# Gated linear attention and a two-level mixture of experts: the attention in a fixed order on every engine

## The chip, the core and the metric

The kernel runs on one core of one Trainium2 chip. The core has a matrix engine (TensorE, PE in the profile; PEld is its weight load), a vector engine (VectorE, DVE), a scalar engine (ScalarE, ACT), a general one (GpSimd, POOL) and a queue engine that issues transfers (SyncE, SP). Each works through its own instructions in order and waits on semaphores of the others. The metric is the device time of one execution in microseconds (us).

## The reference

```python
for t in range(S):                       # gla_recurrent: B 4, H 8, S 768, D 48
    state = alpha[:, :, t, :, None] * state + np.einsum('bhd,bhe->bhde', k[:, :, t], v[:, :, t])
    y[:, :, t] = np.einsum('bhd,bhde->bhe', q[:, :, t], state)
x = y.transpose(0, 2, 1, 3).reshape(B * S, H * D)            # 3072 tokens of 384
g_idx = np.argmax(x @ w_group, axis=1); g_w = softmax(x @ w_group)[g_idx]     # 4 groups
e_idx = np.argmax(x @ w_expert[g], axis=1); e_w = softmax(...)[e_idx]         # 4 experts in a group
out = (g_w * e_w) * (np.maximum(x @ w1[g, e], 0) @ w2[g, e])                  # 384 -> 1024 -> 384
```

## The kernel before, in words

The attention is cut into chunks of 128 tokens: a step n is one chunk of one batch entry, all 8 heads, so there are 4 x 6 = 24 steps (n = 0 to 23), and the state of a batch entry is carried over its 6 steps. Two heads lie together as a pair p (partitions 0 to 47 and 64 to 111), four pairs in all. Inputs come in units of one, two and then three steps.

For a pair of a unit, `decayed` forms the running products of alpha by two scans on VectorE (`back`, L224, and `forth`, L230 and L232) and multiplies them into the keys and queries on GpSimd (`kp`, L227, `qp`, L234). A step then has: `scores` (L245, 8 matrix products into two PSUM banks, one for each head of the pairs, and two causal masks on VectorE, L248); `turned_keys` (transposes L260, copy `kt` on ScalarE, L261); `next_state` (L274, keys by values; the old state added, L281, and scaled by the decay of the chunk, L283, both on VectorE; two copies on ScalarE, L287, that put the heads as blocks on the diagonal of a 112 x 112 matrix); `outputs` (L297, state by queries, whole blocks; L302, masked scores by values; copy `yt` on ScalarE, L306); `to_rows` (L318, the outputs turned to rows of tokens and multiplied by the routers' weights `wr`; logits L321 on VectorE, rows `xr` on ScalarE, L324). An fp32 matrix product is two instructions in the trace, a transpose is one.

After the last step of a batch entry (for the last entry in three parts) `choose` picks group and expert (a chain of small VectorE operations) and `send` counts places and writes the tokens' rows to slots in DRAM, one scatter (L400, an indirect transfer that GpSimd issues) per chunk. Then 16 experts follow, 224 slots each, on the same tiles of weights; their part is not touched.

The order is written as a Python loop with a queue of portions (`later`, `spend`), but the compiler's own scheduler may still reorder the instructions of the attention on every engine. Transfers: SyncE issues `qka` (queries and keys, L194, and alpha, L192, apart) and the weights; ScalarE issues `wr` (L121) and `v` (L201). Scans of a pair write `cq`, of which there are two buffers, so a third scan waits for GpSimd's product of the first.

Of the kernel before, what the change touches and what calls it, by code (L numbers as in the profile page):

```python
# [2 lines left out]

# [21 lines left out]

@with_exitstack
def gla_then_hierarchical_moe(
    ctx: ExitStack,
    tc: tile.TileContext,
    qk_d: bass.AP,  # L30
    al_d: bass.AP,
# [23 lines left out]

    nc = tc.nc
    B, HP, R, SQ = qk_d.shape
    NC = SQ // (2 * P)
# [4 lines left out]
    UC = NC // 2  # L63
    A1 = P + 1
# [56 lines left out]
    nc.scalar.dma_start(out=wr, in_=wr_d)  # L121
# [3 lines left out]
    nc.vector.memset(blank, 0.0)  # L125
    nc.vector.memset(blank.rearrange("p (t w) -> p t w", t=2)[:, :, DM + 1:XW], float(N))
# [6 lines left out]
    nc.vector.tensor_copy(out=xr[:, :, DM + 1], in_=token_f)  # L133
# [13 lines left out]
    with ExitStack() as gla:  # L147
        buf = gla.enter_context(tc.tile_pool(name="buf", bufs=1))
        inp = gla.enter_context(tc.tile_pool(name="inp", bufs=6))
# [8 lines left out]
        state = [buf.tile([R, HP, D], F32, name=f"state{i}") for i in range(2)]  # L158
        blocks = [buf.tile([R, HP, R], F32, name=f"blocks{i}") for i in range(3)]
        for t in state + blocks:  # L160
            nc.vector.memset(t, 0.0)


        units = [(0, 0, 1), (0, 1, 2), (0, UC, UC)]
        units += [(b, c, UC) for b in range(1, B) for c in (0, UC)]
# [19 lines left out]
        def load(u):  # L185
            b, c0, k = units[u]
            o = 2 * k * P
# [10 lines left out]
        def load_v(b):  # L198
            vs[b] = prep.tile([P, NC, DM], F32, name="v")
            for c0, c1 in ((0, 1), (1, NC)) if b == 0 else ((0, NC),):  # L200
                nc.scalar.dma_start(out=vs[b][:, c0:c1].rearrange("p c e -> p (c e)"),  # L201
                                    in_=v_d[b, :, c0 * DM:c1 * DM])
# [35 lines left out]
        def scores(n):  # L238
            u, c = where[n]
            qp, kp, _ = ready[u]  # L240
            sm = work.tile([P, 2, HP, P], F32, name="sm")
            z = [bank() for _ in heads]
            for p in range(HP):
                for i, r in enumerate(heads):
                    nc.tensor.matmul(z[i][:, p * P:(p + 1) * P], lhsT=kp[r, p, c, :],  # L245
                                     rhs=qp[r, p, c, :], start=True, stop=True)
            for i in range(2):
                nc.vector.tensor_tensor(out=sm[:, i], in0=z[i].rearrange("p (h i) -> p h i", h=HP),  # L248
                                        in1=causal[:, None, :].to_broadcast([P, HP, P]),
                                        op=ALU.mult)  # L250
            return sm
# [12 lines left out]
        def next_state(n, kt):  # L264

            u, c = where[n]
            tot = ready[u][2][:, :, c, 0:1]
            z = bank()
            b, bc = divmod(n - 1, NC)
# [8 lines left out]
            old, new = state[(n + 1) % 2], state[n % 2]  # L278
            add = z[0:R, 0:HP * D].rearrange("r (p e) -> r p e", p=HP)
            if bc:  # L280
                nc.vector.tensor_tensor(out=new, in0=old, in1=add, op=ALU.add)  # L281
                add = new
# [5 lines left out]
            return blk  # L288

        def outputs(n, sm, blk):  # L290

            u, c = where[n]
            qp = ready[u][0]
            b, bc = divmod(n, NC)
            z = bank()
            for p in range(HP):
                nc.tensor.matmul(z[0:R, p * P:(p + 1) * P], lhsT=blk[:, p, :], rhs=qp[:, p, c, :],  # L297
                                 start=(p == 0), stop=False, skip_group_check=True)
            for p in range(HP):
                for i, r in enumerate(heads):  # L300
                    h = 2 * p + i
                    nc.tensor.matmul(z[r, p * P:(p + 1) * P],  # L302
                                     lhsT=vs[b][:, bc, h * D:(h + 1) * D], rhs=sm[:, i, p, :],
                                     start=False, stop=True, skip_group_check=True)
# [64 lines left out]
        def send(b, c0, c1):  # L369
# [28 lines left out]
            for c in range(C):  # L398
                yield 1
# [4 lines left out]
                    oob_is_err=False)  # L404

# [7 lines left out]
        later, chosen = deque(), []  # L413

        def portions(gen, done=None):
            def one():
                got = next(gen, one)
                if got is not one:
                    later.insert(got or 0, (0.1 if got else 0.6, one))
                elif done:  # L420
                    done()
            later.append((0.6, one))

        def spend(us):
            while later and us > 0:
                cost, fn = later.popleft()
                us -= cost
                fn()
# [6 lines left out]
        def send_chosen(n):  # L435
            while chosen and n >= FIRST_SENT:
                portions(send(*groups[chosen.pop(0)]))

        FIRST_SENT = 10
        made = 0  # L440

        def make(u):

            nonlocal made
            for p in range(HP):
                later.extend(decayed(u, p))
            made = u + 1

        load(0)
        load(1)  # L450
        load_v(0)
        load(2)
        make(0)
        spend(1e9)
        LAST = B * NC
        sm, blk, yt = scores(0), blocks[0], None
        for n in range(LAST):
# [3 lines left out]
            if n + 1 < LAST and where[n + 1][1] == 0:  # L461
                spend(1e9)
            sm_next = scores(n + 1) if n + 1 < LAST else None
            carry = (n + 1) % NC and n + 1 < LAST
            kt = turned_keys(n) if carry else None
            if n == LAST - 1:
                rows_and_choice(n - 1, yt)
                yt = None
            spend(2.0)
            yt_next = outputs(n, sm, blk)  # L470
            if n + 1 < LAST:
                blk = next_state(n + 1, kt) if carry else blocks[0]
            spend(1.2)
            if yt is not None:
                send_chosen(n)
                rows_and_choice(n - 1, yt)
            spend(1.2)
# [11 lines left out]
            sm, yt = sm_next, yt_next  # L489
        spend(1e9)  # L490
        send_chosen(LAST)
        rows_and_choice(LAST - 1, yt)
        spend(1e9)
        send_chosen(LAST)
        spend(1e9)

# [220 lines left out]
```

## Time and profile before

| | us |
|---|---|
| median of 3 runs (lowest, highest) | 521.55 (520.23, 526.47) |
| the profiled execution | 521.66 |
| its span, first to last instruction | 520.0 |
| TensorE busy | 456.0 (88%) |
| VectorE busy | 174.5 (34%) |
| ScalarE busy | 100.8 (19%) |
| GpSimd busy | 116.2 (22%) |

The rows of the trace are read by their columns: start, busy time, engine, line of the code, operation, output and inputs, shapes, how often; in brackets the idle time just before and what ended it. The shares above are over the whole span; the attention fills about its first 182 us, the experts the rest, and each is to be read by itself.

### The profile page before, as it was taken

What the parts mean: (1) busy time and instruction counts of PE and PEld (TensorE: products, weight loads), DVE (VectorE), ACT (ScalarE), POOL (GpSimd) and SP (SyncE); (2) the same over time, 40 slices, a digit from 0 to 9 for tenths busy, and PEclk for the clock granted to TensorE, in tenths of its full rate; (3) what the DMA queues carried; (4) which work ended last, traced back from release to release, by engine and by line L of the source; (5) the groups of instructions that cost most, each with busy time, mean ns of one, the idle gap of its engine ahead of it and who ended that gap; (6) DMA issues with size and microseconds to landing.
All of it is one profiled execution on the core that took longest, in us unless ns stands there. A gap on an engine that the chain in (4) does not pass through costs nothing. (4 is left out here: it accounts for less than half of the span.)

```text
span 520.0 us, 8206 instructions
## 1 busy us (share of the span) xinstructions
PE 456.0 (88%) x3292; PEld 436.1 (84%) x3292; DVE 174.5 (34%) x460; ACT 100.8 (19%) x211; POOL 116.2 (22%) x146
## 2 busy tenths in 40 slices
PE   1698997868898629999999999999999999999990
PEld 0487877757697629999999999999999999999980
DVE  4779886878585460001001000101001001001000
ACT  0033333232243301111111111111111111111110
POOL 3546423556533220001001001001001001001101
PEclk9999998977899759999999999999999999999995
DMA  8995999877201252546537536537537546443000
GB/s 271 237 248 172 350 298 298 313 241 246 87 2 64 76 161 79 208 150 237 210 139 238 215 133 236 217 132 247 209 128 247 205 141 222 169 140 131 16 9 28
DMA packets 23944, 92.93 MB, mean 179 GB/s; under 512 B 3349, under 2 KB 11658, under 8 KB 19424
## 3 DMA queue, kind: packets, MB, share of 16 engines
q1 hardware_dynamic: 15632, 72.45, 41.7%
q10 hardware_dynamic: 4944, 10.46, 6.1%
q0 software_dynamic: 3328, 9.47, 5.2%
q8 instruction: 27, 0.44, 0.3%
q14 instruction: 13, 0.11, 0.1%
HBM read 77.37 MB, written 15.78 MB: 179 GB/s over the span
## 5 line engine op out<-in xcount | busy, mean ns | idle before, releaser
L519 PE MATMUL bank<-xt_e,w 128*128 128x224 f32 x768 | 152.5, 356 | 0.6 <-DVE dst L627 0.6
L534 PE MATMUL bank<-hT,w 128*128 128x224 f32 x768 | 148.3, 353 | 0.0
L519 PEld LDWEIGHTS bank<-xt_e,w 128*128 128x128 f32 x768 | 145.7, 192 | 1.3 <-DVE dst L627 0.8
L534 PEld LDWEIGHTS bank<-hT,w 128*128 128x128 f32 x768 | 144.1, 190 | 0.0
L548 POOL DMA_INDIRECT out_dram<-yo,dst x32 | 30.5, 952 | 295.3 <-DVE yo L546 199.7
L546 DVE TENSOR_SCALAR yo<-bank,xg 128x384 f32<-128x384 f32 (+1 forms) x32 | 18.2, 611 | 155.3 <-PE bank L544 155.3
L521 ACT ACTIVATE hT<-bank 128x448 f32<-128x448 f32 x64 | 34.8, 544 | 137.8 <-PE bank L519 137.8
L245 PE MATMUL bank<-qp,kp 48*128 48x128 f32 x384 | 33.9, 310 | 18.5 <-POOL qp L234 17.7
L245 PEld LDWEIGHTS bank<-qp,kp 48*128 48x128 f32 x384 | 26.7, 203 | 23.6 <-POOL qp L234 19.6
L297 PE MATMUL bank<-qp,blocks 112*112 112x128 f32 x192 | 31.2, 315 | 14.2 <-ACT blocks L287 14.2
L627 DVE CAST dst<-xg 128x1 int32<-128x1 f32 (+1 forms) x32 | 3.5, 147 | 116.3 <-issue 116.0
L536 ACT COPY yT<-bank 128x448 f32<-128x448 f32 (+1 forms) x32 | 14.1, 439 | 137.1 <-PE bank L534 137.1
L297 PEld LDWEIGHTS bank<-qp,blocks 112*112 112x112 f32 x192 | 27.3, 209 | 15.7 <-ACT blocks L287 15.4
L248 DVE TENSOR_TENSOR sm<-bank,causal 128x512 f32<-128x512 f32 x48 | 30.7, 679 | 7.0 <-PE bank L245 3.8
L318 PE MATMUL bank<-wr,yt 112*128 112x116 f32 x192 | 30.8, 308 | 1.5 <-ACT yt L306 1.0
L302 PE MATMUL bank<-sm,v 128*48 128x128 f32 x384 | 31.0, 306 | 0.0
L400 POOL DMA_INDIRECT slots_d<-xr,place x24 | 23.9, 996 | 30.9 <-DVE place L396 13.3
L227 POOL TENSOR_TENSOR kp<-qka,rev 112x384 f32<-112x384 f32 x24 | 22.5, 936 | 35.9 <-DVE starts L230 15.3
L318 PEld LDWEIGHTS bank<-wr,yt 112*128 112x128 f32 x192 | 26.2, 211 | 3.8 <-issue 1.4
L302 PEld LDWEIGHTS bank<-sm,v 128*48 128x48 f32 x384 | 23.3, 138 | 4.4 <-issue 1.6
L232 DVE TENSOR_TENSOR_SCAN cq<-qka,starts 112x387 f32<-112x387 f32 x24 | 22.9, 956 | 5.7 <-issue 4.2
L234 POOL TENSOR_TENSOR qp<-qka,cq 112x384 f32<-112x384 f32 x24 | 21.9, 912 | 11.8 <-DVE cq L232 10.7
(89 smaller groups left out, 289.6 us busy)
## 6 DMA issues: line engine op xcount, KB each, us to landing
w<-in_w_dram SPq DMA_DIRECT2D x32, 1536.0 KB, 6.6
qka<-in_qk_dram SPq DMA_DIRECT2D x24, 336.0 KB, 7.6
slots_d<-blank SPq DMA_DIRECT2D x1, 5404.0 KB
qka<-in_al_dram SPq DMA_DIRECT2D x24, 169.8 KB, 3.9
v<-in_v_dram ACTq DMA_DIRECT2D x3, 1152.0 KB, 13.9
xg<-slots_d ACTq DMA_DIRECT2D x16, 193.0 KB, 3.8
xg<-slots_d ACTq DMA_DIRECT2D x16, 144.8 KB, 4.1
w<-in_qk_dram SPq DMA_DIRECT2D x4, 336.0 KB, 6.4
```

Of the source, the lines that this page charges most:

```text
L227: nc.gpsimd.tensor_tensor(out=kp, in0=k, in1=rev[:, :, 1:A1], op=ALU.mult)
L232: nc.vector.tensor_tensor_scan(out=flat(cq), data0=a[:, 0:W], data1=st, initial=1.0, op0=ALU.mult, op1=ALU.min)
L245: nc.tensor.matmul(z[i][:, p * P:(p + 1) * P], lhsT=kp[r, p, c, :], rhs=qp[r, p, c, :], start=True, stop=True)
L248: nc.vector.tensor_tensor(out=sm[:, i], in0=z[i].rearrange("p (h i) -> p h i", h=HP), in1=causal[:, None, :].to_broadcast([P, HP, P]), op= ...
L297: nc.tensor.matmul(z[0:R, p * P:(p + 1) * P], lhsT=blk[:, p, :], rhs=qp[:, p, c, :], start=(p == 0), stop=False, skip_group_check=True)
L302: nc.tensor.matmul(z[r, p * P:(p + 1) * P], lhsT=vs[b][:, bc, h * D:(h + 1) * D], rhs=sm[:, i, p, :], start=False, stop=True, skip_group_c ...
L318: nc.tensor.matmul(z[:, p * W:(p + 1) * W], lhsT=yt[:, p, :], rhs=wr[:, p, :], start=True, stop=True)
L400: nc.gpsimd.indirect_dma_start(out=slots_by_tile[b * NC + c0 + c], out_offset=bass.IndirectOffsetOnAxis(ap=place[:, c:c + 1], axis=0), in_ ...
L519: nc.tensor.matmul(z[:, k * n:(k + 1) * n], lhsT=w1[:, dc, f * P:(f + 1) * P], rhs=xt[:, dc, 0:n], start=(dc == 0), stop=(dc == DC - 1))
L521: nc.scalar.activation(out=hT[:, f0:f0 + 2, 0:n], in_=z[:, 0:2 * n].rearrange("p (f t) -> p f t", f=2), func=AF.Relu)
L534: nc.tensor.matmul(z[:, i * n:(i + 1) * n], lhsT=w2[:, f, dc * P:(dc + 1) * P], rhs=hT[:, f, 0:n], start=(f == 0), stop=(f == FC - 1))
L548: nc.gpsimd.indirect_dma_start(out=out, out_offset=bass.IndirectOffsetOnAxis(ap=dst, axis=0), in_=yo[0:n], in_offset=None, bounds_check=N ...
```

## The change

All engines but SyncE keep the written order in the attention (`manual_schedule`). One step is now: transposes, state by queries (`from_before`, L310), keys by values (`gains`, L280), scores by values (`outputs`, L322), the next step's scores (L251), this step's rows (`to_rows`, L339). The state is kept by quarters: a head's 48 x 48 part stands alone, so L310 is eight small products in place of four whole ones, and none in the first step of a batch entry. The second mask is a copy on ScalarE (L256) and a selection on GpSimd (L257). The scaling of the state is four small operations on ScalarE (L298). Alpha, queries and keys come in one transfer; `v` and `wr` are issued by SyncE, `wr` behind the first three units. `qka` has seven buffers, not six. Scatters are queued and one is issued at the end of a step (all at once from step 18 on). Two memsets and a copy move from VectorE to GpSimd.

```diff
+        gla.enter_context(tc.manual_schedule(
+            engines={ENG.PE, ENG.DVE, ENG.Activation, ENG.Pool}))
...
-                nc.sync.dma_start(out=t[:, o:o + k * A1 + 1],
-                                  in_=al_d[b, p, :, c0 * A1:(c0 + k) * A1 + 1])
-                nc.sync.dma_start(out=t[:, 0:o],
-                                  in_=qk_d[b, p, :, 2 * c0 * P:2 * (c0 + k) * P])
+                nc.sync.dma_start(out=t[:, 0:w], in_=qka_d[b, p, :, at:at + w])
...
-            for i in range(2):
-                nc.vector.tensor_tensor(out=sm[:, i], in0=z[i].rearrange("p (h i) -> p h i", h=HP),
-                                        in1=causal[:, None, :].to_broadcast([P, HP, P]),
-                                        op=ALU.mult)
+            nc.vector.tensor_tensor(out=sm[:, 0], in0=z[0], in1=causal[:, None, :].to_broadcast(
+                [P, HP, P]), op=ALU.mult)
+            nc.scalar.copy(out=sm[:, 1], in_=z[1])
+            nc.gpsimd.affine_select(out=sm[:, 1], in_=sm[:, 1], pattern=[[0, HP], [1, P]],
+                                    compare_op=ALU.is_ge, fill=0.0, base=0, channel_multiplier=-1)
...
-            nc.vector.tensor_tensor(out=new, in0=add, in1=tot.to_broadcast([R, HP, D]),
-                                    op=ALU.mult)
-            blk = blocks[1 + n % 2]
-            for r in heads:
-                nc.scalar.copy(out=blk[r, :, r], in_=new[r])
+            nc.vector.tensor_tensor(out=gained, in0=st[:, :, 0:D], in1=add, op=ALU.add)
...
+            for p in range(HP):
+                nc.scalar.activation(out=st[:, p, 0:D], in_=sums[:, p], func=AF.Copy,
+                                     scale=ready[u][2][:, p, c, 0:1])
...
-            for p in range(HP):
-                nc.tensor.matmul(z[0:R, p * P:(p + 1) * P], lhsT=blk[:, p, :], rhs=qp[:, p, c, :],
-                                 start=(p == 0), stop=False, skip_group_check=True)
+            for p in range(HP if n % NC else 0):
+                for i, r in enumerate(heads):
+                    o = slice(64 * i, 64 if i == 0 else R)
+                    nc.tensor.matmul(z[o, p * P:(p + 1) * P],
+                                     lhsT=st[r, p, 0:o.stop - o.start], rhs=qp[r, p, c, :],
+                                     start=(p == 0), stop=False, skip_group_check=True)
...
         load(0)
+        load_v(0, 0, 1)
         load(1)
-        load_v(0)
+        load_v(0, 1, NC)
         load(2)
+        nc.sync.dma_start(out=wr, in_=wr_d)
...
             kt = turned_keys(n) if carry else None
-            spend(2.0)
-            yt_next = outputs(n, sm, blk)
+            spend(1.9, decays, gates)
+            z = from_before(n, st)
+            if carry:
+                sums = grown(n, st, gains(n, kt))
+            yt = outputs(n, sm, z)
+            spend(1.8, decays, gates)
             if n + 1 < LAST:
-                blk = next_state(n + 1, kt) if carry else blocks[0]
-            spend(1.2)
-            if yt is not None:
-                send_chosen(n)
-                rows_and_choice(n - 1, yt)
-            spend(1.2)
+                if where[n + 1][1] == 0:
+                    spend(1e9, decays)
+                sm = scores(n + 1)
+            if carry:
+                st = scaled(n + 1, sums)
+            send_chosen(n)
+            rows_and_choice(n, yt)
+            scatter(1 if n < LAST - NC else NC)
```

**The start.** ScalarE's queue before begins with the routers' weights `wr` and the values `v`; it is beside SyncE's queue of `w1`, `w2` and `qka` (the inputs of the first units lie in the buffers of the experts' weights):

```order
L121 DMA wr<-in_wr_dram 112x464
L201 DMA v<-in_v_dram 128x384
L201 DMA v<-in_v_dram 128x1920
L201 DMA v<-in_v_dram 128x2304
L261 ACT_TABLE_LOAD
```

SyncE's queue of the change begins so (elements of 4 bytes):

```order
L201 DMA w1_129<-in_qka_dram 112x386 x4
L207 DMA v_137<-in_v_dram 128x384
L201 DMA w1_129<-in_qka_dram 112x771
L201 DMA w2_130<-in_qka_dram 112x771 x3
L207 DMA v_137<-in_v_dram 128x1920
L201 DMA w1_131<-in_qka_dram 112x1156 x2
L201 DMA w2_132<-in_qka_dram 112x1156 x2
L481 DMA wr_95<-in_wr_dram 112x464
```

All stand in one queue now, and `wr` is last. On TensorE the change has the products with `wr` of step 0 ahead of all of step 1:

```order
L251 MATMUL bank<-qp,kp 128x128 x8
L339 MATMUL bank<-wr,yt 128x116 x4
L268 MATMUL bank<-ident,kp 128x112 x4
L310 MATMUL bank<-qp,state_126 64x128
L310 MATMUL bank<-qp,state_126 48x128
```

**A step on VectorE.** Before, in a step of the second batch entry (scans are SCALAR_TENSOR_TENSOR):

```order
L230 RECIPROCAL starts_120<-rev_855 112x3
L232 SCALAR_TENSOR_TENSOR cq_857<-qka_523,starts_120 112x387
L224 SCALAR_TENSOR_TENSOR rev_855<-qka_526,starts_120 112x387
L281 TENSOR_TENSOR state1_124<-state0_123,bank_833 112x192
L230 RECIPROCAL starts_120<-rev_855 112x3
L283 TENSOR_TENSOR state1_124<-state1_124,rev_629 112x192
L232 SCALAR_TENSOR_TENSOR cq_858<-qka_526,starts_120 112x387
L321 TENSOR_REDUCE lg_779<-bank_846 128x20
L224 SCALAR_TENSOR_TENSOR rev_855<-qka_529,starts_120 112x387
L230 RECIPROCAL starts_120<-rev_855 112x3
L232 SCALAR_TENSOR_TENSOR cq_859<-qka_529,starts_120 112x387
L248 TENSOR_TENSOR sm_860<-bank_861,causal_75 128x512
```

Now, all of step 3:

```order
L230 SCALAR_TENSOR_TENSOR rev_440<-qka_270,starts_121 112x387
L236 RECIPROCAL starts_121<-rev_440 112x3
L238 SCALAR_TENSOR_TENSOR cq_441<-qka_270,starts_121 112x387
L290 TENSOR_TENSOR gained_124<-state1_126,bank_466 112x192
L230 SCALAR_TENSOR_TENSOR rev_440<-qka_272,starts_121 112x387
L236 RECIPROCAL starts_121<-rev_440 112x3
L238 SCALAR_TENSOR_TENSOR cq_442<-qka_272,starts_121 112x387
L254 TENSOR_TENSOR sm_491<-bank_492,causal_75 128x512
L342 TENSOR_REDUCE lg_262<-bank_509 128x20
```

Two pairs of scans stand in each of the first two steps of a unit, with one addition to the state between them; the scaling is gone and one mask is left.

**The scatters on GpSimd.** Before, those of the second batch entry stand together between two units' products:

```order
L227 TENSOR_TENSOR kp_1302<-qka_939,rev_1303 112x384
L234 TENSOR_TENSOR qp_1301<-qka_939,cq_1307 112x384
L400 DMA slots_d_69<-xr_103,place_1333 49152x386 x6
L227 TENSOR_TENSOR kp_1504<-qka_1145,rev_1505 112x384
L227 TENSOR_TENSOR kp_1504<-qka_1148,rev_1505 112x384
```

Now, from the end of step 17 to the end of step 19:

```order
L421 DMA slots_d_69<-xr_102,place_1488 49152x386
L233 TENSOR_TENSOR kp_1539<-qka_1154,rev_1540 112x384
L240 TENSOR_TENSOR qp_1538<-qka_1154,cq_1541 112x384
L233 TENSOR_TENSOR kp_1539<-qka_1156,rev_1540 112x384
L240 TENSOR_TENSOR qp_1538<-qka_1156,cq_1542 112x384
L257 AFFINE_SELECT sm_1582<-sm_1582 128x512
L421 DMA slots_d_69<-xr_102,place_1488 49152x386 x5
L233 TENSOR_TENSOR kp_1539<-qka_1158,rev_1540 112x384
L240 TENSOR_TENSOR qp_1538<-qka_1158,cq_1543 112x384
L233 TENSOR_TENSOR kp_1539<-qka_1160,rev_1540 112x384
L240 TENSOR_TENSOR qp_1538<-qka_1160,cq_1544 112x384
L257 AFFINE_SELECT sm_1669<-sm_1669 128x512
```

One scatter of the second batch entry goes out at the end of step 17, and its other five stand together in step 18, ahead of two pairs' products and of the selection for step 20.

## Rows read from the trace of the kernel before

**Rows 1.** Busy by stretch: length, PE, PEld, DVE, ACT, POOL, clock, DMA share, GB/s.

```profile
5.00:10.00 5.00, 0.80 (x4) 0.50 (x4) 1.30 (x4) 1.28 (x1) 0.56 (x2) 1.00 1.06 323
...
43.78:144.35 100.57, 83.85 (x966) 74.36 (x965) 78.67 (x175) 30.85 (x71) 49.75 (x55) 0.90 0.78 258
```

**Rows 2.** Timeline of TensorE in step 18: start, busy us, line, tiles, count.

```profile
143.26 1.16 PE L245 MATMUL bank<-qp,kp 48*128 48x128 f32 x16
...
144.35 0.60 PE L260 MATMUL bank<-ident,kp 112*128 112x112 f32 x4
...
144.79 1.04 PE L297 MATMUL bank<-qp,blocks 112*112 112x128 f32 x8
...
145.76 1.08 PE L302 MATMUL bank<-sm,v 128*48 128x128 f32 x16
...
146.67 0.61 PE L274 MATMUL bank<-v,kt 128*64 128x48 f32 x16
...
147.21 1.15 PE L318 MATMUL bank<-wr,yt 112*128 112x116 f32 x8
...
148.29 1.16 PE L245 MATMUL bank<-qp,kp 48*128 48x128 f32 x16
```

**Rows 3.** Instructions of VectorE by line: count, busy us, mean ns.

```profile
L248 DVE TENSOR_TENSOR sm<-bank,causal 128x512 f32<-128x512 f32 x48 | 30.7, 679 | 7.0 <-PE bank L245 3.8 <-PE bank L260 1.4 <-remote 1.2
...
L283 DVE TENSOR_TENSOR state<-state,rev 112x192 f32<-112x192 f32 x16 | 6.9, 432 | 0.4
L281 DVE TENSOR_TENSOR state<-state,bank 112x192 f32<-112x192 f32 x16 | 5.5, 342 | 15.2 <-issue 8.6 <-PE bank L274 6.7
```

**Rows 4.** Timeline of VectorE in step 18, a scan pair.

```profile
143.06 0.94 DVE L224 TENSOR_TENSOR_SCAN rev<-qka,starts 112x387 f32<-112x387 f32 x1
...
143.91 0.22 DVE L321 TENSOR_REDUCE lg<-bank 128x20 f32<-128x80 f32 x1
...
145.20 0.93 DVE L224 TENSOR_TENSOR_SCAN rev<-qka,starts 112x387 f32<-112x387 f32 x1
```

**Rows 5.** Instructions of ScalarE by line, mean ns after the busy time.

```profile
L306 ACT COPY yt<-bank 112x512 f32<-112x512 f32 x24 | 14.1, 587 | 44.3 <-PE bank L302 38.8 <-PE bank L318 4.5 <-remote 1.1
...
L324 ACT COPY xr<-bank 128x384 f32<-128x384 f32 x24 | 11.5, 480 | 14.5 <-DVE lg L321 14.3
L261 ACT COPY kt<-bank 128x448 f32<-128x448 f32 x20 | 10.6, 532 | 26.0 <-PE bank L260 21.3 <-remote 4.7
```

**Rows 6.** Instructions of GpSimd by line.

```profile
L227 POOL TENSOR_TENSOR kp<-qka,rev 112x384 f32<-112x384 f32 x24 | 22.5, 936 | 35.9 <-DVE starts L230 15.3 <-DVE seen L383 8.5 <-DVE rev L224 5.5
...
L96 POOL TENSOR_SCALAR_AFFINE_SELECT causal<-causal 128x128 f32<-128x128 f32 x1 | 0.3, 285 | 0.0
```

**Rows 7.** Timeline, all engines: end of the first burst of scatters.

```profile
104.75 0.98 POOL L400 DMA_INDIRECT slots_d<-xr,place  x1 [0.30 <-issue]
105.74 0.93 POOL L234 TENSOR_TENSOR qp<-qka,cq 112x384 f32<-112x384 f32 x1
...
106.70 0.96 DVE L232 TENSOR_TENSOR_SCAN cq<-qka,starts 112x387 f32<-112x387 f32 x1 [4.24 <-issue]
```

**Rows 8.** Timeline: TensorE after a pause in step 22.

```profile
170.18 1.34 PE L274 MATMUL bank<-v,kt 128*64 128x48 f32 x16 [3.10 <-issue]
...
171.45 2.06 PE L318 MATMUL bank<-wr,yt 112*128 112x116 f32 x8
```

**Rows 9.** Timeline: the last copy of outputs and the last scatter.

```profile
178.43 0.59 ACT L306 COPY yt<-bank 112x512 f32<-112x512 f32 x1 [1.68 <-PE bank L302]
...
184.75 1.06 POOL L400 DMA_INDIRECT slots_d<-xr,place  x1 [0.30 <-DVE ends L577]
```

**Rows 10.** Timeline of GpSimd and VectorE around two products of ranks.

```profile
95.95 0.92 POOL L227 TENSOR_TENSOR kp<-qka,rev 112x384 f32<-112x384 f32 x1 [1.28 <-DVE rev L224]
96.05 0.93 DVE L393 TENSOR_TENSOR rk<-rk,picked 128x96 f32<-128x96 f32 x1
...
126.87 0.26 DVE L393 TENSOR_TENSOR rk<-rk,picked 128x96 f32<-128x96 f32 x1
```

More of the change, by code (lines that the diff above doesn't have):

```diff
@@ L23, with units_of @@
 HUGE = 3e38
+def units_of(B, NC):
+    h = NC // 2
+    return [(0, 0, 1), (0, 1, h - 1), (0, h, NC - h)] + [
+        (b, c, k) for b in range(1, B) for c, k in ((0, h), (h, NC - h))]
 @with_exitstack
@@ L63, in gla_then_hierarchical_moe @@
     UC = NC // 2
+    units = units_of(B, NC)
     A1 = P + 1
@@ L186, in load @@
             b, c0, k = units[u]
-            o = 2 * k * P
+            at = sum(k_ * (2 * P + A1) + 1 for b_, c_, k_ in units if b_ == b and c_ < c0)
+            w = k * (2 * P + A1) + 1
             for p in range(HP):
@@ L397, in send, with scatter @@
             count(C - 1)
-            for c in range(C):
-                yield 1
+            def scatter(c):
                 nc.gpsimd.indirect_dma_start(
@@ L404, in send @@
                     oob_is_err=False)
+            outgoing.extend(partial(scatter, c) for c in range(C))
         groups = {b * NC + NC - 1: (b, 0, NC) for b in range(B - 1)}
@@ L410, in gla_then_hierarchical_moe, with spend @@
             groups[(B - 1) * NC + c1 - 1] = (B - 1, c0, c1)
-        later, chosen = deque(), []
+        decays, gates, chosen, outgoing = deque(), deque(), [], deque()
         def portions(gen, done=None):
             def one():
-                got = next(gen, one)
-                if got is not one:
-                    later.insert(got or 0, (0.1 if got else 0.6, one))
+                if next(gen, one) is not one:
+                    gates.appendleft((0.7, one))
                 elif done:
                     done()
[L422 to L428, printed above, removed]
+            gates.append((0.7, one))
+        def spend(us, *queues):
+            for queue in queues:
+                while queue and us > 0:
+                    cost, fn = queue.popleft()
+                    us -= cost
+                    fn()
         def rows_and_choice(n, yt):
@@ L436, in send_chosen, with scatter @@
             while chosen and n >= FIRST_SENT:
-                portions(send(*groups[chosen.pop(0)]))
-        FIRST_SENT = 10
-        made = 0
+                sending = send(*groups[chosen.pop(0)])
+                next(sending)
+                portions(sending)
+        def scatter(most):
+            while outgoing and most > 0:
+                outgoing.popleft()()
+                most -= 1
+        FIRST_SENT = 9
         def make(u):
-            nonlocal made
             for p in range(HP):
-                later.extend(decayed(u, p))
-            made = u + 1
+                decays.extend(decayed(u, p))
         load(0)
+        load_v(0, 0, 1)
         load(1)
-        load_v(0)
+        load_v(0, 1, NC)
         load(2)
+        nc.sync.dma_start(out=wr, in_=wr_d)
         make(0)
-        spend(1e9)
+        spend(1e9, decays)
         LAST = B * NC
-        sm, blk, yt = scores(0), blocks[0], None
+        sm, st, sums = scores(0), None, None
         for n in range(LAST):
@@ L488, in gla_then_hierarchical_moe @@
                 load_v(n // NC + 1)
[L489 to L495, printed above, removed]
+        while gates or chosen:
+            send_chosen(LAST)
+            spend(1e9, gates)
+            scatter(NC)
     mp = ctx.enter_context(tc.tile_pool(name="moe", bufs=2))
```

96 lines of the change are left out of this document (51 added, 45 removed).

## The prediction

> **What bounds the kernel now.** I read the busy shares first, then the timeline of the attention, where every edit lies; the experts behind it keep their code and their weights' transfers, so I let them move as a block. In the attention I ask of each stretch which engine is full. Steps 3 to 17 begin at 43.78 and end at 144.35 us [rows 1]: 6.70 us a step. VectorE is busy 78.67 us of these 100.57, 5.2 a step, TensorE 83.85. What a step costs when TensorE alone limits it is seen from step 18 on, where the inputs of all units are nearly done: from one start of the scores (L245) to the next 5.03 us, at the full clock [rows 2]. So 1.7 us of each step before is not TensorE's work. It goes to VectorE, which holds the scans, both masks and the state, and to bursts of scatters: after the six scatters of a batch entry the next product waits on GpSimd, the scan that needs its buffer starts as that product ends, and VectorE has stood 4.24 us [rows 7].
>
> **The change, part by part.**
>
> *VectorE.* It loses 24 masks of 0.68 us and the scaling of the state, 16 of 0.43 and 4 from PSUM [rows 3]; three memsets of `blocks` and the memset of `blank` go at the start. A pair of scans takes 2.14 us from one backward scan to the next, a logits' sum of 0.22 inside [rows 4]. A step with two pairs is then 2 x 2.14 + 0.34 (addition to the state) + 0.68 (mask) = 5.3 us, with hand-overs **5.4**. Of the 15 steps ten have two pairs. The gates' portions (small operations) fall into the third step of a unit, where no scans are.
>
> *The scaling's reads.* The scaling read two SBUF tiles. An operation with two SBUF inputs took 0.93 us when it began 0.1 us after a GpSimd product, and 0.26 with GpSimd idle [rows 10]. So each such operation can lose 0.67 us to GpSimd, and 16 of them go; I take nothing for it, since the mean of 0.43 already holds what they lost. The Trainium skill's GPSIMD Engine Reference (Specifications) says that GpSimd's SBUF interfaces are shared with VectorE, with contention where a VectorE instruction has two SBUF inputs. The trace agrees; by that rule the change, which gives GpSimd more to do, could lose on the operations left, and that is the last rival below.
>
> *TensorE.* State by queries was 8 instructions in 0.97 us, next to 16 row-halves (scores) in 1.09 and 16 column-halves (L302) in 0.91 [rows 2]. The quarters are 16 instructions that use half the rows and half the columns. I take 0.95, as their nearest neighbours; if no two ran at once they would take 16 x 0.121 = 1.94. Four first steps do without them. The sum of a step stays 0.44 + 0.95 + 0.54 + 0.92 + 1.09 + 1.08 = 5.0 us, 4.05 for the last of a batch entry, which has neither transposes nor keys by values.
>
> *ScalarE.* It gains the copy of a mask's bank (0.59 as L306, about the same size [rows 5]) and four scalings of 48 columns. From 0.480 at 384 and 0.587 at 512 columns the slope is 0.84 ns, so about 0.20 each; I take 0.24, with 0.20 and 0.48 as ends. With `kt` 0.53, `yt` 0.59, `xr` 0.48 that is 3.2 us of a step, so it isn't full. But in the fixed order `kt` waits behind mask copy, scalings and `xr`: scores end, 0.1 + 0.59 + 0.96 + 0.48 + 0.53 = 2.7 us pass, while TensorE has 1.08 + 0.44 + 0.95 = 2.5 to do. So a step that VectorE doesn't limit costs about **5.3**.
>
> *GpSimd.* A product is 0.94 us, a selection of 128 columns 0.285 [rows 6], a scatter 0.98 + 0.30 = 1.28 [rows 7]. The new selection has 512 columns: no less than 0.285, no more than 4 x 0.285 = 1.14; with a fixed part I take 0.84. Three steps: 8 x 0.94 + 3 x 0.84 + 3 x 1.28 = 13.9 us against 16.1 for VectorE, so it is not full, and a selection late by 1.5 us is still in time.
>
> *The start.* One queue now, in order of need. Ahead of and with `wr` lie 691,712 + 196,608 + 1,381,632 + 983,040 + 2,071,552 + 207,872 bytes (the shapes in the queue's rows) = 5.53 MB; at 323 GB/s [rows 1] this is 17.1 us, so with issue and landing `wr` is there at about 19.5; at 258 GB/s it would be 23. Unit 0 lands near 5 us and step 0 passes early, but its products with `wr` stand in TensorE's queue ahead of step 1, and its logits' sum in VectorE's ahead of unit 2's scans. So **a new wait** holds both until 19.5. TensorE comes out of it at the lower of its two levels (1.2 GHz): after 3.10 us of idling, products that take 1.08 took 2.06 and keys by values 1.34 [rows 2, 8]. Step 1 begins at 21.6 and costs 7.6 at that level; step 2 costs 7.3, because step 3's scores want unit 2's last product straight after its scans (0.22 + 2 x 2.14 + 0.34 + 0.94, then scores' rest and rows). Step 3 begins at 36.5, now 43.78.
>
> *Steps 3 to 17.* 10 x 5.4 + 2 x 5.3 + 3 x 4.6 (last steps, 4.05 and a wait for the mask) = 78.4 us. Step 18 begins at 114.9, now 144.35: **29 us ahead**.
>
> *Steps 18 to 23.* Here the scatters are not one a step. In step 18 five stand together behind selection 19, which ends 6.8 us into the step (four products 3.7 behind the first scans): 121.7 + 5 x 1.28 + 4 x 0.94 + 0.84 = 132.7 is the end of selection 20. The outputs of step 20 could have begun at 127.7; they wait 5.0, and three groups at the lower clock cost 2.8 more. Steps 18, 19, 20 take 5.2 + 5.4 + 13.8 (the products of `send` in it), step 21 6.0, step 22 5.3: step 23 begins at 150.6. Six more scatters behind selection 22 delay selection 23 to 155.0, where 151.6 was due: 3.4 and 1.8 for the clock. `yt` of step 23 is at 157.0, now 178.43. From there to the last scatter it is 6.3 us now [rows 9] and 7.4 at the lower clock, so 164.4 in place of 184.75. **Sum: 20.3 us.** The profiled execution took 521.66 (span 520.0), 0.1 above the median of 521.55: 521.66 - 20.3 = **501.4 us**.
>
> **Rivals.**
>
> 1. *The forecast*: chance 0.55, its own range 494 to 509.
>
> 2. *The two late stalls don't come*, or `wr` lands by 15 us: more of the 29 us is kept. For it: before, most of two bursts passed beside other work. Against it: the order puts selection 20 behind five scatters. 501.4 - 7.8 - 5.2 + 1 = 489. Chance 0.15.
>
> 3. *Quarters one by one*: 1.94 in place of 0.95, TensorE 6.0 a step, above VectorE's 5.4: 0.6 x 12 and the rest in steps 18 to 23, 8 in all: 509. Against it, scores in halves show 0.068 us an instruction and not 0.121. Chance 0.10.
>
> 4. *No gain: the fixed order waits where a scheduler filled in.* Before, an engine took what was ready; now a late instruction stops all behind it. If a step lost 0.9 us to this, 6.3 a step, over 20 steps: 501 + 18 = 519. For it: ScalarE's chain above is already 0.2 too long, and scans come in front of the addition to the state. Chance 0.13.
>
> 5. *Slower: GpSimd becomes the bound.* Place: the selection, in its queue with products and scatters. It decides from 3s + 7.5 + 3.8 = 16.1, s = 1.6 us; the whole gain is gone at 6.7 a step, s = 2.9. At 4 us steps with scatters take 7.8, without 6.5, where 5.2 is the mean above: 7 x 2.6 + 8 x 1.3, and some 8 more in the two late queues: 501 + 36 = 537. Against it: 0.285 for a quarter of the columns. Chance 0.04.
>
> 6. *Slower: GpSimd holds VectorE.* `choose` and `send` have eight operations with two SBUF inputs, for six parts 48. If each lost 0.67 us: 32 us, 534. Against it: before, GpSimd was busy half of the stretch (49.75 of 100.57 us [rows 1]), and few were hit. Chance 0.03. This is the rule of the GPSIMD Engine Reference in the Trainium skill taken at its hardest.
>
> **The numbers.** The likeliest is the forecast: 501.4. Below 489 I leave 0.1, above 518 the rest of 0.2: 489 to 518 takes in `wr` between 15 and 23 us (-4.5 to +3.5), the selection at 0.285 or 1.14 (-2 to +3), scalings to 0.48 (+6) and quarters one by one (+8). About 2% (10.4 us) can be told from no change. Faster by more (below 511.1): nearly all of 1, all of 2, most of 3: 0.77. Within 2%: 0.16, from 3 and 4. Slower by more than 2% (above 532): 0.07.
>
> **What would show it.** Right: TensorE's first products with `wr` near 20 us, just after that transfer; two pairs of scans and a step of 5.3 to 5.6 us between steps 3 and 17; a pause of TensorE of 4 us or more after step 19 that ends with a selection, and one after step 22; the last scatter near 165. Wrong: a step above 6 us with VectorE under 80% busy (rival 4); L310's sixteen in 1.9 us (rival 3); GpSimd without idle time in steps 11 to 17 (rival 5); two-input operations of `choose` at 0.9 us (rival 6); a first expert that begins later than the last scatter allows, as when its weights or rows are late, would spoil the sum from another side.

## The result

The changed kernel took 507.89 us (median of 4 runs, 504.26 to 509.79), the kernel before 523.46 beside it: a ratio of 0.9695, 95% interval 0.9608 to 0.9783. It is faster, by 15.6 us where 20.3 were forecast. Its profiled execution took 509.79 us (span 508.1), against 521.66 (520.0): 11.9 of difference. The 4 us between the two differences are within the spread of the runs; steps are compared in the traces. Ratios, here and below, are of the fast runs alone and medians of all runs, so the two can differ by up to 0.4%.

Busy by stretch, first with the columns of [rows 1]: the start, and steps 3 to 17 by the same two marks as there (transposed keys of step 3, of step 18).

```profile
5.00:10.00 5.00, 4.01 (x20) 2.63 (x20) 3.14 (x9) 0.59 (x1) 2.60 (x7) 1.00 0.99 259
20.00:25.00 5.00, 0.00 (x0) 0.00 (x0) 0.00 (x0) 0.00 (x0) 0.00 (x0) 0.50 1.04 244
42.08:121.31 79.23, 76.21 (x1054) 65.58 (x1053) 64.79 (x144) 41.18 (x110) 51.97 (x62) 0.96 0.95 291
```

Fifteen steps take 79.23 us in place of 100.57: 5.28 a step. TensorE is busy 96% of it, VectorE 82%. At 121.31 the kernel is 23.0 us ahead. But from 20 to 25 us no engine did anything, and of the 23.0 us only 13.7 are left at the first expert, 179.37 (193.10).

The timeline at the start, where the products of step 0 with `wr` (L339) stand ahead of step 1's transposed keys (L268) and, on VectorE, the logits' sum (L342) ahead of unit 2's scans (L230):

```profile
25.86 2.03 PE L339 MATMUL bank<-wr,yt 112*128 112x116 f32 x8 [8.29 <-DMA wr<-in_wr_dram]
...
27.68 0.95 PE L268 MATMUL bank<-ident,kp 112*128 112x112 f32 x4
...
27.93 0.24 DVE L342 TENSOR_REDUCE lg<-bank 128x20 f32<-128x80 f32 x1 [9.63 <-PE bank L339]
...
28.09 0.95 DVE L230 TENSOR_TENSOR_SCAN rev<-w,starts 112x387 f32<-112x387 f32 x1
```

What answers to [rows 2 to 6], from the groups by line and form of 42 to 121 us (count, busy us, mean ns, then idle time ahead and its releasers):

```profile
L238 DVE TENSOR_TENSOR_SCAN cq<-qka,starts 112x387 f32<-112x387 f32 x20 | 19.2, 959 | 2.1
...
L298 ACT ACTIVATE state<-gained,rev 112x48 f32<-112x48 f32 x44 | 11.1, 326 | 0.0
...
L254 DVE TENSOR_TENSOR sm<-bank,causal 128x512 f32<-128x512 f32 x15 | 10.1, 676 | 6.6 <-PE bank L251 6.6
L257 POOL TENSOR_SCALAR_AFFINE_SELECT sm<-sm 128x512 f32<-128x512 f32 x15 | 9.5, 636 | 13.8 <-ACT sm L256 12.5 <-DVE sm L254 1.3
L256 ACT COPY sm<-bank 128x512 f32<-128x512 f32 x15 | 8.8, 586 | 8.5 <-PE bank L251 8.5
```

VectorE now waits 6.6 us for scores (L254 <- L251) and GpSimd 13.8, nearly all of it for a copy of them (L256): in these steps the others wait for TensorE. The sixteen quarters took 1.08 us at the full clock (four scalings on ScalarE 1.01):

```profile
49.95 1.01 ACT L298 ACTIVATE state<-gained,rev 112x48 f32<-112x48 f32 x4
...
50.73 1.08 PE L310 MATMUL bank<-qp,state 48*64 48x128 f32 x16
```

The first late pause, in steps 19 and 20, behind five scatters from 127.77 ("remote" means that the wait ended with no instruction that the profile shows):

```profile
132.18 0.59 ACT L327 COPY yt<-bank 112x512 f32<-112x512 f32 x1 [4.47 <-remote]
...
132.82 1.15 PE L339 MATMUL bank<-wr,yt 112*128 112x116 f32 x8 [2.37 <-ACT yt L327]
...
136.04 1.96 PE L310 MATMUL bank<-qp,state 48*64 48x128 f32 x16 [1.64 <-ACT state L298]
...
137.48 0.71 POOL L257 TENSOR_SCALAR_AFFINE_SELECT sm<-sm 128x512 f32<-128x512 f32 x1
...
138.62 0.45 PE L322 MATMUL bank<-sm,v 128*48 128x128 f32 x1
```

TensorE waits for `yt` and for the state. Selection 20 (L257) ends at 138.19, before TensorE gets to the outputs that need it (L322), so in this trace the selection doesn't hold it.

The second late pause answers to [rows 7, 8]. Timeline of step 22 and 23, with six scatters from 148.67:

```profile
150.37 1.05 PE L322 MATMUL bank<-sm,v 128*64 128x128 f32 x15
...
153.11 0.35 DVE L290 TENSOR_TENSOR gained<-state,bank 112x192 f32<-112x192 f32 x1 [3.08 <-remote]
...
155.14 0.98 POOL L421 DMA_INDIRECT slots_d<-xr,place  x1 [0.30 <-issue]
157.46 0.59 ACT L327 COPY yt<-bank 112x512 f32<-112x512 f32 x1 [7.64 <-remote]
157.61 0.69 DVE L254 TENSOR_TENSOR sm<-bank,causal 128x512 f32<-128x512 f32 x1 [4.15 <-remote]
...
158.09 2.06 PE L339 MATMUL bank<-wr,yt 112*128 112x116 f32 x8 [4.59 <-ACT yt L327]
...
158.60 0.63 POOL L257 TENSOR_SCALAR_AFFINE_SELECT sm<-sm 128x512 f32<-128x512 f32 x1 [2.48 <-ACT sm L256]
```

The outputs (L322) are done by 151.4, and their copy by ScalarE begins at 157.46, though ScalarE does nothing else. VectorE's addition waits in the same way for products done at 150.5. TensorE's pause ends with `yt` (4.59). The selection, which the forecast had as the cause, is not what TensorE waits for here, and began late only because its own input, ScalarE's copy, was late. What answers to [rows 9]:

```profile
164.05 0.59 ACT L327 COPY yt<-bank 112x512 f32<-112x512 f32 x1 [2.74 <-PE bank L322]
...
171.43 0.98 POOL L421 DMA_INDIRECT slots_d<-xr,place  x1 [1.04 <-issue]
```

### The profile page after: what moved, and what is told of

Its sections match the earlier page's. It is cut to its first block, busy times and chain, and to the rows that moved or that the text cites. A ratio compares the mean times of both kernels' runs of the same rounds, so it can differ in the third digit from the quotient of the medians.

```text
span 508.1 us, 8473 instructions
## 1 busy us (share of the span) xinstructions
PE 449.5 (88%) x3420; PEld 426.6 (84%) x3420; DVE 157.1 (31%) x410; ACT 116.6 (23%) x275; POOL 132.4 (26%) x173
## 5 line engine op out<-in xcount | busy, mean ns | idle before, releaser
L339 PE MATMUL bank<-wr,yt 112*128 112x116 f32 x192 | 30.2, 305 | 15.8 <-DMA wr<-in_wr_dram 8.3
L251 PE MATMUL bank<-qp,kp 48*128 48x128 f32 x384 | 32.6, 304 | 10.2 <-POOL qp L240 9.8
L339 PEld LDWEIGHTS bank<-wr,yt 112*128 112x128 f32 x192 | 25.7, 208 | 18.4 <-issue 8.4
L251 PEld LDWEIGHTS bank<-qp,kp 48*128 48x128 f32 x384 | 26.1, 200 | 16.5 <-POOL qp L240 11.3
L322 PE MATMUL bank<-sm,v 128*48 128x128 f32 (+1 forms) x384 | 32.8, 302 | 0.5 <-POOL sm L257 0.4
L322 PEld LDWEIGHTS bank<-sm,v 128*48 128x48 f32 (+1 forms) x384 | 25.8, 145 | 2.0 <-POOL sm L257 1.2
L327 ACT COPY yt<-bank 112x512 f32<-112x512 f32 x24 | 14.1, 586 | 55.2 <-PE bank L322 41.5
L310 PE MATMUL bank<-qp,state 48*48 48x128 f32 (+1 forms) x320 | 25.2, 304 | 1.6 <-ACT state L298 1.6
L310 PEld LDWEIGHTS bank<-qp,state 48*48 48x48 f32 (+1 forms) x320 | 19.5, 142 | 5.1 <-ACT state L298 2.2
```

The lines of the kernel that those rows point to most:

```text
L310: nc.tensor.matmul(z[o, p * P:(p + 1) * P], lhsT=st[r, p, 0:o.stop - o.start], rhs=qp[r, p, c, :], start=(p == 0), stop=False, skip_group_ ...
L322: nc.tensor.matmul(z[o, p * P:(p + 1) * P], lhsT=vs[b][:, bc, h * D:h * D + o.stop - o.start], rhs=sm[:, i, p, :], start=(p == 0 and bc == ...
L339: nc.tensor.matmul(z[:, p * W:(p + 1) * W], lhsT=yt[:, p, :], rhs=wr[:, p, :], start=True, stop=True)
```

## The experiments

The theory to test: the gain of a step needs both the order and VectorE's relief; the missing part went into `wr` at the start and into rows of scatters late. Rivals: another load is next in line, the late pauses belong to their steps, or one part of the change does all of it. The runs below fell on three chips. Beside them the kernel before took 507.64 us on one, 521.64 and 522.8 on another, 509.08 on a third, so across chips only ratios are compared.

**The changed kernel again.** No edit.

> The changed kernel once more, on the chip that also runs the three variants, so that they are compared with it and not across chips: 0.97 of the kernel before, about 508 us.

504.96 us against 507.64: 0.9913 (0.9877 to 0.9948), not the 0.97 expected. On this chip the change is worth 0.9%, not 3%. Its trace, late steps:

```profile
128.46 0.59 ACT L327 COPY yt<-bank 112x512 f32<-112x512 f32 x1 [1.76 <-PE bank L322]
...
132.27 4.39 DVE L370 TENSOR_TENSOR oh<-oh,mx 128x120 f32<-128x120 f32 x1
...
136.47 0.68 POOL L257 TENSOR_SCALAR_AFFINE_SELECT sm<-sm 128x512 f32<-128x512 f32 x1
...
137.20 1.90 PE L322 MATMUL bank<-sm,v 128*48 128x128 f32 x14 [4.27 <-POOL sm L257]
...
150.52 0.59 ACT L327 COPY yt<-bank 112x512 f32<-112x512 f32 x1 [1.72 <-PE bank L322]
...
155.11 0.65 POOL L257 TENSOR_SCALAR_AFFINE_SELECT sm<-sm 128x512 f32<-128x512 f32 x1
...
155.81 1.07 PE L322 MATMUL bank<-sm,v 128*48 128x128 f32 x14 [1.84 <-POOL sm L257]
```

No wait is "remote" here. What is left is the forecast's mechanism alone: after five scatters and four products TensorE waits 4.27 us for selection 20 (forecast 5.0), after six it waits 1.84 for selection 23 (3.4). `yt` of step 23 is at 156.98 (164.05), the first expert at 172.07 (179.37). A third time, on a chip where the kernel before took 522.8:

> The changed kernel a third time, beside the next two, for a trace from the same chip. If the kernel before takes about 522 us beside it, the waits that no instruction explains come back in its bursts (ScalarE 4 us or more before yt of step 19 or of step 22) and the ratio is 0.97; if it takes about 507, they are gone and the ratio is 0.99.

507.51 us, 0.9719 (0.9627 to 0.9811), and the waits are back: `yt` of step 19 after 5.19 us "remote", of step 22 after 7.59. From `yt` of step 21 to that of step 22 pass 11.29 us there and 5.42 above. In step 20 the two pauses coincide (`yt` at 139.03 and 139.20), so in these two traces the waits cost the changed kernel some 6 us, once. (The medians on the two chips are only 2.55 us apart.)

**The kernel before, again.**

> The kernel before once more, for its trace. In the second trace of the changed kernel two waits of ScalarE (4.5 and 7.6 us) that no instruction explains were gone, and the kernel before took 507.64 us beside it, not 523.46. Theory A (the kernel before lost time to such waits too, in its three bursts of six scatters, and loses less of it here): the 4.24 us of VectorE before the scan at 106.70, the 4.7 at 136.9 and the 4.7 of ScalarE at 169.6 are gone or under 1.5 us, the first expert begins at 177 to 182 (193.10), and the steps between bursts keep their 5.0 to 6.4 us. Theory B (the waits belong to the kernel, and the 16 us lie in the experts, or in the start): the first expert at 190 to 193, the experts 313 us (326.9).

This run fell on a chip where it took 519.79 us, and the waits were all there, so theory A was not tried; that stays open. (The first expert began at 191.26, as B has it, but the experts took 326.8 us, not 313.) The same three places:

```profile
104.13 0.96 DVE L232 TENSOR_TENSOR_SCAN cq<-qka,starts 112x387 f32<-112x387 f32 x1 [4.23 <-issue]
...
132.93 0.59 ACT L306 COPY yt<-bank 112x512 f32<-112x512 f32 x1 [4.62 <-remote]
...
167.81 0.53 ACT L261 COPY kt<-bank 128x448 f32<-128x448 f32 x1 [4.76 <-remote]
```

The first is of another kind than the other two: in [rows 7] the scan starts as the GpSimd product behind the scatters ends (105.74 + 0.93), so there it is GpSimd's queue that VectorE waits for.

**Scatters or a busy GpSimd?** In place of each scatter from step 18 on:

```diff
+                for _ in range(len(outgoing)):
+                    held.append(outgoing.popleft())
+                    nc.gpsimd.memset(filler, 0.0)
+                    nc.gpsimd.memset(filler[:, 0:580], 0.0)
```

> From step 18 on each scatter is replaced by two memsets on GpSimd of 1.28 us together, in the same place of its queue, and all of these scatters go at the end, where they cost about 20 us; what counts is the trace up to yt of step 23. Theory A (a row of scatters does more than occupy GpSimd: TensorE's completions reach the other engines late while it lasts): no wait of ScalarE before yt of step 19 and of step 22 (4.5 and 7.6 us in the changed kernel), step 23's outputs follow selection 23 at once, and its yt comes 5 us earlier, at 158 to 160. Theory B (it is only the selection that waits in GpSimd's queue, as forecast): the same pauses with the fillers, yt of step 23 at 163 to 165.

> As the variant with fillers before: from step 18 on two memsets of 1.28 us in place of each scatter, these scatters at the end. The first time it ran where the changed kernel itself had no waits without a reason, which told nothing. Theory A (rows of scatters delay what TensorE reports to the others): where the changed kernel beside it shows such waits in steps 19 and 22, this one shows none before its scatters begin, and only the wait for selection 20 and a shorter one for 23 are left. Theory B (a busy GpSimd is enough): the waits of 4 to 8 us come with the fillers as well.

The first ran on the chip without such waits (525.15 us) and told nothing. The second (528.57 us, one execution) ran on the chip of the third trace above:

```profile
128.84 0.59 ACT L327 COPY yt<-bank 112x512 f32<-112x512 f32 x1 [1.76 <-PE bank L322]
...
138.12 1.94 PE L322 MATMUL bank<-sm,v 128*48 128x128 f32 x14 [4.80 <-POOL sm L257]
...
153.35 0.59 ACT L327 COPY yt<-bank 112x512 f32<-112x512 f32 x1 [1.72 <-PE bank L322]
...
183.58 0.59 ACT L327 COPY yt<-bank 112x512 f32<-112x512 f32 x1 [9.54 <-remote]
```

With GpSimd as busy, and no scatter, `yt` of steps 19 and 22 wait 1.76 and 1.72 us, for TensorE itself. The last line is from the same execution: in the row of 14 held scatters, from 163.55 on, the wait is back, 9.54 us before `yt` of step 23. Theory A: it takes the scatters. The wait for the selection, 4.80, stays. (The times behind 153.35 can't be compared with the changed kernel's: VectorE waited 20.4 us for the buffer of ranks that the held scatters still had to read.) Why scatters do it, and on some chips only, no run shows.

**Parts undone.** VectorE gets its two jobs back; the order by hand goes; all scatters at once:

```diff
-            nc.scalar.copy(out=sm[:, 1], in_=z[1])
-            nc.gpsimd.affine_select(out=sm[:, 1], ...
+            nc.vector.tensor_tensor(out=sm[:, 1], in0=z[1], in1=causal[...], op=ALU.mult)
...
-                nc.scalar.activation(out=st[:, p, 0:D], in_=sums[:, p], func=AF.Copy, ...
+            nc.vector.tensor_tensor(out=st[:, :, 0:D], in0=sums, op=ALU.mult, in1=...
```

> The second mask and the scaling of the state stand on VectorE again, as in the kernel before; all else is as in the changed kernel, the fixed order too. Theory A (VectorE was what a step waited for, and its relief is what shortened the steps): a step with two pairs of scans 2 x 2.14 + 0.34 + 2 x 0.68 + 0.43 = 6.4 us in place of 5.1, ten of them, so 10 to 14 us slower than the changed kernel, 515 to 519 where that takes 505. Theory B (TensorE sets the step, and VectorE has 14 us left of the 79 of steps 3 to 17): 2 to 4 us slower, since the scans only move into its idle time.

523.55 us, 1.0028 (0.9994 to 1.0063).

```diff
-        gla.enter_context(tc.manual_schedule(
-            engines={ENG.PE, ENG.DVE, ENG.Activation, ENG.Pool}))
```

> The changed kernel without its order by hand: the same instructions on the same engines, put in order by the scheduler as in the kernel before. Theory A (the order is a part of the gain: scores of the next step ahead of the rows, state ahead of them on ScalarE): 5 to 12 us slower than the changed kernel, steps 3 to 17 at 5.6 us or more. Theory B (the order costs, as the rival with 0.9 us a step had it): 10 to 18 us faster, steps 3 to 17 at 4.4 us or somewhat above.

527.02 us, 1.0119 (1.0083 to 1.0156). Both beside 521.64. Steps 3 to 17 of the first and of the second, between the same marks:

```profile
44.17:132.60 88.43, 75.40 (x1054) 65.44 (x1053) 75.48 (x173) 21.58 (x44) 44.40 (x47) 0.96 0.82 268
```

```profile
40.13:144.29 104.16, 88.32 (x1055) 75.47 (x1054) 64.77 (x147) 41.46 (x108) 57.59 (x69) 0.85 0.77 254
```

With VectorE's jobs back, the order still makes 88.43 us of 100.57, with VectorE and TensorE 85% busy each; two-pair steps after step 3 take 5.9 to 6.2 (6.4 expected). That lead is lost later, beside rows of five and nine scatters (5.97 and 3.57 us "remote" on ScalarE). Without the order, VectorE's relief gives nothing (104.16): it is busy only 64.77 us, and the engines wait for each other. Both together: 79.23. In all the two are 16.0 and 19.5 us slower than the changed kernel's 507.51 on this chip, more than theory A of either expected.

Two limits of this comparison. Both variants keep the rest of the change (the quarters, the one transfer, seven buffers), so the kernel before is not quite the fourth case beside these three. And without the order by hand six scatters stand in a row again, twice in these steps (from 85.47 and from 123.86), with waits of 3.63 and 4.32 us "remote" beside them: a part of what the order gives is that it keeps the scatters apart. How large a part, no run on this chip separates; the next one has the order with the rows of six, on another chip.

```diff
-            scatter(1 if n < LAST - NC else NC)
+            scatter(NC)
```

> One part of the change undone: no scatter waits for a step of its own, all that are ready go at once in every step, so six stand in a row in step 12 and six in step 18, as in the kernel before. Theory A (the forecast's: a row of six holds the four products and the selection behind it, 7.7 us of GpSimd, and on a chip where TensorE's completions come late beside scatters, ScalarE and VectorE besides): the two rows cost 4 to 7 us each at steps 12, 13 and 18, 19, the row of five in step 19 is no longer there, so 3 to 8 us slower than the changed kernel, a ratio of 0.98 to 0.99 where that has 0.97. Theory B (in steps 12 to 18 GpSimd has room, so that such a row passes beside other work): the same time within 2 us.

514.82 us against 509.08: 1.0105 (1.0037 to 1.0173), so 1.9% above the changed kernel's 0.9913 on a chip that, like this one, shows no "remote" waits; the changed kernel itself did not run on this chip. That is some 10 us, above the 3 to 8 expected: theory A, with a price too low. The rows of six in steps 12 and 18 each hold a selection. Timeline of the first:

```profile
95.66 0.98 POOL L421 DMA_INDIRECT slots_d<-xr,place  x1 [0.30 <-issue]
96.66 0.93 POOL L233 TENSOR_TENSOR kp<-qka,rev 112x384 f32<-112x384 f32 x1
...
100.10 0.63 POOL L257 TENSOR_SCALAR_AFFINE_SELECT sm<-sm 128x512 f32<-128x512 f32 x1
...
100.79 1.94 PE L322 MATMUL bank<-sm,v 128*48 128x128 f32 x14 [5.15 <-POOL sm L257]
```

This first row cost nearly 10 us: steps 13 and 14 took 13.3 and 7.0 us, in the trace on the other chip 5.1 and 5.3. TensorE's products after the pause run at the lower clock (granted clock 0.50 from 101 to 107 us; L322 1.94 us, else 1.07), and that is in the price.

**The start, and fewer scatters in a row.**

```diff
         load_v(0, 0, 1)
+        nc.sync.dma_start(out=wr, in_=wr_d)
         load(1)
```

> The transfer of wr stands ahead of the inputs of unit 1 instead of behind those of unit 2. Theory A (the start is late because wr lands behind 5.3 MB that move at about 240 GB/s, and TensorE and VectorE hold everything behind the products with wr): the first product with wr at about 14.5 us (25.86), step 1 at about 18.5 (27.68), step 3 at 31 to 33 (42.08), bounded by unit 2's scans; later steps keep their length, so the time falls by 8 to 10 us, to 498 to 500. Theory B (the inputs of units 3 and 4 are the next thing that is late, so that the lead is given back within steps 3 to 9): step 3 at 32, but a step of 7 us or more before step 9, and the time falls by 2 to 4 us only.

496.85 us, 0.9801 (0.9752 to 0.9851): less than the changed kernel beside it by 8.1 us of the medians, 5.7 of the ratios, and 6.5 at the first expert. The first product with `wr` came at 17.52, no longer held by `wr` but by the scores ahead of it, step 1 at 19.37, step 3 at 34.71 (41.76 there): a little later than expected. At step 12 it is 9.95 ahead, and there TensorE waits for the next values:

```profile
83.53 0.92 PE L280 MATMUL bank<-v,kt 128*64 128x48 f32 x15 [3.05 <-DMA v<-in_v_dram]
```

By step 18 6.25 are left. Nearer to theory A by the time, at or below the lower end of its 8 to 10 us, with a piece of B at another place than it named.

```diff
-            scatter(1 if n < LAST - NC else NC)
+            scatter(1 if n < LAST - NC else 2)
```

> From step 18 on at most two scatters a step instead of all that are ready; what is left goes at the end (10 there instead of 3). Theory A (the two late pauses are made by the bursts of five and six): the pause after step 19 (132.2 to 138.6 us) shrinks by 4 to 5 us, that after step 22 by 6 to 8, yt of step 23 at about 152 to 154 (164.05), the last scatter at 164 to 166 (171.43), the time 500 to 503. Theory B (the pauses belong to these steps, as from products, selections or code that is loaded there, and not to the bursts): yt of step 23 at 162 to 164, the last scatter at 174 to 176, the time 511 to 513.

498.91 us, 0.9817 (0.9764 to 0.9871): 6.1 us less by the medians, 4.9 by the ratios. From step 18 to `yt` of step 23 29.1 us (36.7 in the changed kernel beside it); the row of ten at the end takes a part back, so that the first expert begins only 3.7 us earlier. Theory A, on the chip without "remote" waits. Then together:

```diff
+            scatter(1 if n < LAST - NC else 2 if n < LAST - 3 else 3)
+            if n % NC == 0 and n and n // NC + 1 < B:
+                load_v(n // NC + 1)
```

> wr ahead of unit 1's inputs, the values of the next batch entry two thirds of an entry earlier and ahead of the inputs of unit 6 (in the variant with wr early, TensorE had waited 3.05 us for them in step 12), and from step 18 on two scatters a step, three from step 21. Theory A (these pauses are separate, and each is worth what it took): 8 for wr, 6 for the scatters, 3 for the values, so 17 us less than the changed kernel, 488 where that takes 505; last scatter at 148 to 150. Theory B (they share time: a lead gained at the start is given back where the inputs of a unit come late): 494 to 497.

492.84 us, 0.9453 (0.9415 to 0.9491): 14.7 us below the changed kernel's 507.51 on this chip, so most of theory A's 17. `yt` of step 22 came after 3.39 us "remote", beside a row of three. With two everywhere:

> The variant with three moves, but never more than two scatters a step, so none stand in rows of three before the end; ten stand in a row at the end (nine there). Theory A (three in a row are enough for such a wait, as in its step 22, where ScalarE waited 3.39 us): yt of step 22 without a wait, yt of step 23 at 141 to 143 (145.99), the last scatter at 152 to 154 and the time 2 us lower, 490 to 491 where the other took 493. Theory B (the row at the end takes it back, yt of step 23 or its logits being held there): the same time or up to 2 us more.

491.24 us against 522.8, 0.9391 (0.9335 to 0.9448): the best, 31.6 us below the kernel before and 16.3 below the changed kernel's 507.51 beside it. From the 492.84 it can't be told apart by the ratios, whose intervals overlap; what the trace shows is that `yt` of step 22 no longer waits longer than usual (1.97, for the outputs themselves), as theory A has it; the row of ten at the end does hold step 23:

```profile
136.80 0.58 ACT L327 COPY yt<-bank 112x512 f32<-112x512 f32 x1 [1.97 <-PE bank L322]
...
143.55 0.58 ACT L327 COPY yt<-bank 112x512 f32<-112x512 f32 x1 [3.82 <-remote]
...
152.44 0.98 POOL L421 DMA_INDIRECT slots_d<-xr,place  x1 [1.04 <-issue]
```

## Why the prediction was right, and where it was not

- **Direction and range** hold: 507.89 lies in 489 to 518 and in the likeliest case's own 494 to 509.
- **The start** is the step that was mis-sized. The new wait on `wr` came, in both queues, at the lower clock, as said; but `wr` was used at 25.86, not 19.5, and step 3 began at 42.08, not 36.5. The 323 GB/s of [rows 1] were not reached: 259 and 244 above. By the other row, 258, I had 23 (with the same 2.4 us for issue and landing it is 23.8), and even that was short: by 25.8 us the core had moved 6.1 MB, at 235 GB/s on average, and not the 5.53 that lie ahead of and with `wr`. Seven more transfers of inputs were issued behind `wr` from 11.28 on; that they took their share ahead of its landing is likely, but no run shows it. 5.6 of the 7 us that the last scatter came later than forecast (171.43 for 164.4) are this. Moving one transfer gave back 5.7 to 8.1.
- **Steps 3 to 17**: 79.23 for 78.4. Two errors cancel, which is luck: two-pair steps took 5.0 to 5.3 (5.4 forecast; TensorE works through them nearly without idling, so its 5.0 sets them, not VectorE), and step 3 took 8.2 at the lower clock, which I had not seen coming. VectorE's own share of such a step, from one logits' sum to the next, is the forecast's 5.3 in most of them; the third step of a unit makes up for its lag. Quarters 1.08 (0.95), scalings 0.25 each of a train (0.24), selection 0.64 (0.84).
- **Steps 18 to 20**: the row of five in front of selection 20 is right, and selection 20 ended 16.9 us after step 18 began (17.8 forecast). But in the first trace the pause did not end with it, as I had said it would: the late `yt` and the state held TensorE until then (2.37 and 1.64 us). Without "remote" waits it was the selection, 4.27 us (5.0 forecast), and with two scatters a step 0.44.
- **Steps 22 and 23**: 3.4 and 1.8 us were put down to the selection. Where no wait is "remote", it was 1.84; in the first trace the pause was made by what TensorE had finished reaching ScalarE late, of which I knew nothing. The kernel before had it too: the pause of [rows 8] follows a copy (`kt`, 169.60) that came after 4.66 us "remote", while [rows 7] is GpSimd's queue, as I read it. So the sum of these steps agrees by luck: from step 18 to `yt` of step 23 I had 42.1 us and the first trace has 42.7, but the selections alone, on the chip without such waits, make it 36.7.
- **What I let move as a block**, the experts, took 328.7 us for 326.9: 1.8 of the miss.
- **Rivals.** 2 did not come: both pauses did. 3 is out (1.08, not 1.94). 4 has the wrong sign: without the order by hand nothing is gained (1.0119). 5 is out: GpSimd idles 13.8 us of 79 ahead of its selections. 6 came in single operations only: of `choose`'s with 120 columns (0.28 us) L362 took 0.77, 0.76 and 1.56 in the first trace (the last at 136.13), and L370 4.39 above, there while the outputs waited for the selection anyway.
- **What I could not see**: that much of the difference depends on the chip. Against a kernel before of 507.64 us the same change gives 0.9%. There the time, 504.96, would still lie in my range, but not the gain of 20.3 us that it was worked out from; that the gain came near to it where it was measured first is in part luck.

## What to carry to other kernels

Taking work off the engine that looks full gave nothing until the queues were in an order that let the others use it, and the order alone lost its lead later; try the two together before dropping either. In a hand-made order, a transfer that one small early product needs belongs ahead of the large ones, since everything behind that product in its queue waits with it. Spread scatters one or two a step: here a row of five or six held what followed in GpSimd's queue for 4 to 5 us, and on some chips the other engines besides. And compare two versions on one chip: here the chip made as much difference to the kernel before as the change did.

## What the runs showed of the hardware

- While three or more scatters follow each other, ScalarE and VectorE go on late with what TensorE has finished, on some chips: `yt` waited 7.64, 5.19, 7.59 and 9.54 us beside rows of five and more, 3.39 beside a row of three, where 1.7 to 2.0 is usual. On another chip the same program had no such wait (1.76 and 1.72), and with memsets of about the same length there was none. TensorE's own trains break into pieces meanwhile (the scores of step 23 into three, from 151.36 to 153.50). The kernel before took 507.64 and 509.08 us on two chips whose traces show no such waits, 521.64 and 522.8 on one whose traces do; that the waits make this difference is not shown, since no trace of it is from one of the quicker chips.
- One operation of VectorE with two SBUF inputs (L370, else 0.28 us) took 4.39 us, from 132.27 to 136.66, beside four GpSimd products in a row, 132.93 to 136.51. The Trainium skill's GPSIMD Engine Reference (Specifications) names such contention; the trace agrees, and shows in this one place that it can last about as long as the products do.
